# One set of phase multiples, high rows by turning forward and back, late numerators copied by ScalarE, and spectra of u in two-bank PSUM tiles

## The chip, the cores and the metric

The kernel runs on one core of one Trainium2 chip. The metric is the device time of one execution in microseconds: the median of three runs of the kernel before is 298.48 us (298.02 to 301.67). Beside the runs there is one profiled execution with a trace of every instruction; it took 299.34 us and its span, from the first to the last instruction, is 297.6 us. The core's engines are TensorE (PE, whose weight loads are listed as PEld), VectorE (DVE), ScalarE (ACT), GpSimd (POOL) and SyncE (SP); the last two do little but issue transfers here. Each engine works through its own list of instructions in order and waits on semaphores for the others.

## The reference

Two independent parts are computed, and their outputs stand side by side in one array of 2048 x 896 in bf16.

Part A is linear attention with feature maps: sequence length 2048, width 448, 16 heads of 28.

```
q, k, v = split(x @ wqkv)
phi_q = [softmax(q @ w_phi), softmax(-(q @ w_phi))]      # the same for phi_k
kv, z   = phi_k^T v, sum of phi_k over the sequence
o       = (phi_q kv) / (phi_q z + 1e-6);   out_A = o @ wo
```

Part B is a state-space convolution: 448 channels, 256 states, length 2048.

```
K[d, l] = Re sum_n C[d, n] exp(dt[d] A[d, n] l) dt[d] B[d, n]       # l = 0 .. 2047
y       = causal convolution of u with K along l, by FFT of length 4096;  out_B = y + u * Dskip
```

## The kernel before

**The table of powers.** The 448 channels are cut into 8 chunks (k = 0 to 7) of 56. In a chunk 128 states lie on partitions, and a row has 112 columns: 56 channels by two halves of the states (`COLS`). The kernel K is evaluated only at such l as bf16 can hold, each as a sum of a high part from `HI` (32 values: multiples of 32 up to 1920) and a low part from `LO` (50 values between -15 and 128). For each chunk the steps are:

- `phases` (L663): PE multiplies the log-magnitudes (`AT`) or the angles (`TH`), as bf16 pairs of value and remainder, with scaled identities (`PID`), one for each entry of `DIAG`. There are two sets of eight multiples, so two PSUM tiles of two banks (`arg`, of which two exist) for the magnitudes and two for the angles, each by 16 matmuls of 128x112. ACT then evaluates groups of rows out of PSUM by `EVALS` and, for the negative rows, `MIRROR`: `dampings` takes exponentials into `E` (11 instructions, 49 rows), `rotations` takes sines and cosines into `W` (16 instructions, 2 x 34 rows). The scale of an instruction (1, 2, 4, 8) turns one set of multiples into others.
- `damp` (L700): DVE multiplies the rotations with the exponentials, in two pieces (3360 and 7616 columns); `neg` flips a sign in 1680 columns, on DVE or ACT.
- `hi_tables` (L714): DVE builds the 32 high rows in `U`, as complex products in bf16. Rows 0 to 3 are copied from `H`. Level 1 multiplies them by the 128th power (rows 4 to 7), level 2 all eight by the 256th power (rows 8 to 15), and levels 3 to 5 use the 512th. A level is one multiply of both factors' parts at once, then a subtraction and an addition.
- `build_k` (L734): PE contracts `U` with `W` into PSUM, and ACT or DVE copies the result into a table of K values.

`W`, `E` and `U` have two buffers, so a chunk's work overlaps that of the next two.

**From the table to the output.** DMAs scatter the table into rows by position (`scatter_k`, issued on SP, POOL and ACT), PE transforms it (`kernel_spectrum`, with tables that are loaded from DRAM by `load_f` into a ring of buffers, and copies by ACT or DVE into `SK`), DVE multiplies it with the spectrum of u (`conv_group`), and PE transforms back (`inverse`), for three channel groups one after the other: group 0 is chunks 0 to 3, group 1 chunks 4 and 5, group 2 chunks 6 and 7. The spectrum of u is computed early (`signal_spectrum`, L621): in steps of 448 columns it is transformed into one-bank PSUM tiles (`mm`), copied by ACT or DVE, and sent to DRAM (`SUd`); `load_su` brings it back, one load for each group.

**Attention.** `key_pair` and `key_end` build kv and z. `query` (L808) handles four blocks of 512 positions, sc = 0 to 3. For each of a block's four tiles PE makes the numerators of both softmax halves in a two-bank `arg` tile, DVE multiplies them out of PSUM (f32) by the scale `SC`, one factor for each head of 28 columns, into `on` (bf16, 896 columns), and PE adds the halves, transposes and projects.

**What sets the order.** Every operation is a unit with its engines and dependencies. Nothing is scheduled at build time: the string `ORDER` (L98) lists all 1451 units, each with the engine that issues it (P, V, A, G and S for PE, DVE, ACT, POOL and SP), and `PLACES` (L168) says which PSUM pool a tile comes from. An engine's list is the order of its units in that string. Copies, sign flips and transfers may stand on either of several engines. The costs written beside the units were used to find the string and change nothing else.

## Time and profile before

| | |
|---|---|
| Median of three runs | 298.48 us (298.02 to 301.67) |
| Profiled execution | 299.34 us, span 297.6 us |
| PE busy | 263.8 us (89% of the span) |
| DVE busy | 275.7 us (93%) |
| ACT busy | 247.4 us (83%) |
| POOL busy | 71.5 us (24%) |
| Transfers | 35.20 MB, mean 118 GB/s |
| Granted TensorE clock | 0.992 |

Busy time is the time in which at least one instruction of the engine runs. An instruction's own duration includes the wait for its last results, which overlaps the next instruction on the same engine; the sum of durations is therefore more than the busy time. In a row of a group stand, after the bar, the busy time, the mean duration of one instruction, and the idle time of the engine before them with what ended it. Line numbers are those of the helpers that issue: L345 is `tt` (two-operand DVE work), L358 is `act` (activations), L362 is `acopy`, L368 is `copy`, L378 is `mm`, L393 is `dma`, L712 is the sign flip.

### The profile page before, as it was taken

The page shows a single profiled execution, that of the slowest core. Times are in us where ns is not written, and L with a number is a line of the kernel's source. Part 1 is how long each engine was busy: PE and PEld are TensorE (multiplying, and loading weights), DVE is VectorE, ACT ScalarE, POOL GpSimd, SP SyncE. Part 2 cuts the span into 40 slices and gives each one's busy share as a digit, 9 for nine tenths or more (in the row PEclk, how much of TensorE's full clock was granted, in tenths as well). Part 3 has the DMA queues.
Part 4 walks back from the last instruction along what each step waited for, and adds up shares of the span by engine and source line. Part 5 has one row for each costly group of instructions (what it writes and reads, how often), then busy time and mean ns, then how long its engine had stood idle before and what let it go on. Part 6 is the DMA issues. An engine that isn't in the chain of part 4 may idle for free. (4 is left out here: it accounts for less than half of the span.)

```text
span 297.6 us, 10488 instructions
## 1 busy us (share of the span) xinstructions
PE 263.8 (89%) x4536; PEld 215.4 (72%) x4536; DVE 275.7 (93%) x317; ACT 247.4 (83%) x470; POOL 71.5 (24%) x123
## 2 busy tenths in 40 slices
PE   7788999999989899989997879899778889899994
PEld 3455676786685687868775659688667688889983
DVE  2799999999999999899999999899989999999990
ACT  2989999999999999999699999999999825452331
POOL 4031222502011101000298000029910048600000
PEclk9999999999999999999997999999999999999998
DMA  6976544542022101021044300316986878775025
GB/s 197 315 207 199 165 103 133 117 65 54 10 67 50 45 4 46 4 48 50 6 69 84 85 17 4 87 43 130 261 303 175 256 232 220 196 244 173 18 79 170
DMA packets 40520, 35.20 MB, mean 118 GB/s; under 512 B 22078, under 2 KB 37687, under 8 KB 40347
## 3 DMA queue, kind: packets, MB, share of 16 engines
q1 hardware_dynamic: 34999, 30.53, 35.1%
q0 software_dynamic: 4288, 3.97, 6.8%
q8 instruction: 35, 0.57, 0.8%
q10 hardware_dynamic: 1188, 0.04, 0.2%
q14 instruction: 10, 0.08, 0.1%
HBM read 24.28 MB, written 7.34 MB: 106 GB/s over the span
## 5 line engine op out<-in xcount | busy, mean ns | idle before, releaser
L378 PEld LDWEIGHTS <-sbuf 128*32 128x32 bf16 (+4 forms) x4312 | 203.8, 118 | 70.8 <-issue 32.6
L345 DVE TENSOR_TENSOR sbuf<-sbuf 128x896 bf16<-128x896 bf16 (+6 forms) x197 | 216.7, 1135 | 5.6 <-ACT sbuf L358 4.1
L378 PE MATMUL mm<-sbuf 128*32 128x50 bf16 (+10 forms) x2257 | 143.8, 267 | 14.6 <-ACT sbuf L368 6.5
L358 ACT ACTIVATE sbuf<-arg 128x448 bf16<-128x448 f32 (+4 forms) x238 | 125.9, 644 | 1.4 <-PE arg L378 0.7
L378 PE MATMUL kb<-sbuf 128*32 128x50 bf16 (+9 forms) x1153 | 74.3, 246 | 3.4 <-ACT sbuf L368 1.0
L393 POOL DMA_DIRECT2D sbuf<-sbuf x80 | 47.8, 623 | 113.3 <-ACT sbuf L368 95.6
L378 PE MATMUL arg<-sbuf 128*128 128x112 bf16 (+4 forms) x902 | 62.4, 220 | 7.7 <-ACT sbuf L358 5.9
L368 ACT CAST sbuf<-mm 128x448 bf16<-128x448 f32 (+4 forms) x96 | 54.3, 585 | 16.7 <-PE mm L378 14.5
L368 ACT CAST sbuf<-kb 128x448 bf16<-128x448 f32 (+3 forms) x42 | 23.3, 593 | 19.3 <-PE kb L378 16.1
L393 POOL DMA_DIRECT2D SUd<-sbuf x24 | 17.9, 749 | 61.5 <-ACT sbuf L368 42.9
L358 ACT ACTIVATE sbuf<-mm 112x512 bf16<-112x512 f32 x36 | 21.2, 649 | 0.3 <-PE mm L378 0.3
L345 DVE TENSOR_TENSOR sbuf<-arg,sbuf 128x896 bf16<-128x896 f32 (+1 forms) x21 | 20.3, 973 | 0.6 <-PE mm L378 0.2
L358 ACT ACT_TABLE_LOAD x14 | 18.0, 1283 | 1.4 <-PEq L1106 1.2
L358 ACT ACTIVATE sbuf<-sbuf 128x896 f32<-128x896 f32 (+2 forms) x12 | 11.7, 1017 | 1.8 <-DMA sbuf<-in_B_log_dt_dram 1.8
L712 ACT ACTIVATE sbuf<-sbuf 128x1680 bf16<-128x1680 bf16 x6 | 10.5, 1756 | 0.0
L785 PEld LDWEIGHTS <-sbuf 112*128 112x128 bf16 x128 | 7.3, 97 | 1.8 <-issue 1.0
L368 DVE COPY sbuf<-kb 112x512 bf16<-112x512 bf16 (+2 forms) x16 | 6.8, 434 | 1.4 <-PE kb L574 0.9
L345 DVE TENSOR_TENSOR sbuf<-mm,sbuf 128x896 bf16<-128x896 bf16 (+1 forms) x13 | 7.4, 566 | 0.6 <-PE mm L785 0.5
L368 DVE CAST sbuf<-mm 128x448 bf16<-128x448 f32 (+1 forms) x11 | 6.6, 597 | 1.0 <-PE mm L378 0.7
L574 PEld LDWEIGHTS <-sbuf 128*112 128x112 bf16 x64 | 4.9, 129 | 3.3 <-issue 2.8
L574 PE MATMUL kb<-sbuf 128*112 128x128 bf16 x64 | 5.7, 219 | 1.7 <-ACT sbuf L368 1.5
L362 ACT CAST sbuf<-sbuf 128x1792 bf16<-128x1792 f32 (+1 forms) x5 | 7.1, 1429 | 0.0
(37 smaller groups left out, 63.3 us busy)
## 6 DMA issues: line engine op xcount, KB each, us to landing
sbuf<-const SPq DMA_DIRECT2D x36, 224.0 KB
sbuf<-const SPq DMA_DIRECT2D x7, 512.0 KB
sbuf<-in_B_u_dram SPq DMA_DIRECT2D x6, 448.0 KB
sbuf<-in_A_x_dram SPq DMA_DIRECT2D x4, 448.0 KB
out_dram<-sbuf SPq DMA_DIRECT2D x16, 112.0 KB
sbuf<-SUd SPq DMA_DIRECT2D x1, 1792.0 KB
sbuf<-SUd SPq DMA_DIRECT2D x2, 896.0 KB
out_dram<-sbuf SPq DMA_DIRECT2D x8, 224.0 KB
```

Source lines behind the costliest of these rows:

```text
L345: lambda: nc.vector.tensor_tensor(out=at(out_), in0=at(a), in1=at(b), op=op), [whose(a), whose(b)], [out_])
L358: lambda: nc.scalar.activation(at(out_), at(a), func, scale=scale, bias=bias),
L362: plan.add({"ACT": 0.09 + count(out_) * 0.833e-3}, lambda: nc.scalar.copy(at(out_), at(a)), [whose(a)], [out_])
L368: lambda e: (nc.scalar.copy if e == "ACT" else nc.vector.tensor_copy)(at(out_), at(a)), [whose(a)], [out_])
L378: nc.tensor.matmul(out_, lhsT=lhsT, rhs=rhs, start=start, stop=stop, **kw)
L393: plan.add({e: own[e] for e in engs}, lambda e=engs[0]: QUEUES[e].dma_start(out=out_, in_=in_, **kw), r, w, lat=lat, load=pieces / 16000 * ...
L574: mms(p, [lambda t, j=j, x=x: nc.tensor.transpose(t[:, j, :], x[:, 112 * j:112 * j + 112], ident[:, :]) for j in range(4)], 0.4, [x, ident ...
L712: lambda en: nc.scalar.mul(m, m, -1.0) if en == "ACT" else nc.vector.tensor_scalar_mul(m, m, -1.0), [m], [m])
L785: mms(pt, [lambda t, i=i, s=s, c=c: nc.tensor.transpose(t[:, s, 112 * c:112 * c + 112], EKT[:, s, c, 128 * i:128 * i + 128], id112) for s ...
```

## The change

- `phases` uses one set of eight multiples (1, 3, ... 15) in one PSUM tile. The other rows come from larger scales of the instructions on ACT (up to 128), in more and shorter groups: 15 exponentials and 2 x 11 sines for a chunk.
- `hi_tables` first makes rows 8 to 11 from rows 0 to 3 by the 256th power. A second product of these four rows with the 128th power serves twice: with one set of signs it gives rows 12 to 15 and, turned the other way, rows 4 to 7, which are then scaled by the new tile `BACK` (the inverse of the squared magnitude, made once at the start).
- In `query`, blocks from `N_EARLY` = 2 on take another way: ACT copies the numerators out of PSUM into `on`, and DVE multiplies `on` in place by a bf16 scale.
- `signal_spectrum` uses two-bank `arg` tiles of 2 x 448 columns, with one copy each.
- The order of all units (now 1517) and the places of the PSUM tiles are new, and with them the engine of many copies, sign flips and transfers. `gather` has other costs written beside it.

```diff
--- before.py
+++ after.py
@@ -21,6 +21,7 @@
 SSM_N = 256
 
 N_IDLE = 24
+N_EARLY = 2
 N_LO = 50
 N_HI = 32
 NQ = 14
@@ -30,17 +31,15 @@
 QC = 2 * COLS
 NCOL = NCHK * COLS
 HW = D_MODEL // 2
-DIAG = [[1, 3, 5, 7, 9, 11, 13, 15], [4, 8, 12, 16, 20, 28, 24, 32]]
-EVALS = [[(1, 0, 8, 16, 2, 0), (2, 0, 4, 17, 4, 0), (4, 4, 2, 34, 1, 0), (8, 4, 4, 42, 2, 0)],
-         [(1, 0, 4, 19, 4, 0), (1, 4, 4, 32, 1, 1), (2, 4, 4, 38, 1, 2), (4, 4, 4, 43, 2, 2)]]
-MIRROR = [[(-1, 0, 8, 0, 2, 0), (-2, 0, 4, 1, 4, 0)], [(-1, 0, 3, 3, 4, 0)]]
+DIAG = [1, 3, 5, 7, 9, 11, 13, 15]
+EVALS = [(1, 0, 8, 16, 2), (2, 0, 4, 17, 4), (4, 0, 2, 19, 8), (4, 2, 4, 32, 1), (8, 0, 1, 23, 1), (8, 1, 7, 38, 1),
+         (16, 0, 2, 31, 5), (16, 2, 2, 45, 1), (32, 0, 2, 37, 10), (64, 0, 1, 48, 1), (128, 0, 1, 49, 1)]
+MIRROR = [(-1, 0, 8, 0, 2), (-2, 0, 4, 1, 4), (-4, 0, 2, 3, 8), (-8, 0, 1, 7, 1)]
 ZERO = 15
 LO = [0] * N_LO
-for _ds, _ev, _mi in zip(DIAG, EVALS, MIRROR):
-    for _f, _e, _n, _r, _s, _kind in _ev + _mi:
-        for _i in range(_n):
-            _j = (_i, 4 * (_i // 2) + _i % 2, 2 * (_i % 2) + _i // 2)[_kind]
-            LO[_r + _s * _j] = _f * _ds[_e + _i]
+for _f, _e, _n, _r, _s in EVALS + MIRROR:
+    for _i in range(_n):
+        LO[_r + _s * _i] = _f * DIAG[_e + _i]
@@ -89,85 +88,88 @@
...
-ORDER = ("23G 42P 31P 43P 30P 33P 46P 0A 48A 49V 8G 191G 32..."
...
-PLACES = ("kmmmmkmmkmmkmmkkmkkmkkmkkkkkmmkmmkmmkkmkmkmmmkkk..."
...
+ORDER = ("0A 48A 3S 1S 2S 4S 8G 23G 13S 25P 46P 36P 30P 32P..."
...
+PLACES = ("kkkkmmkkkmkmmkmmkmmmmkkmmkkmmmkkmmamkkmmakmkakak..."
...
@@ -398,12 +400,13 @@
     oEND = oF + 61672
     oT2 = oEND + 4096
     DSK = sb("DSK", [128, D_MODEL], BF16, oDSK)
-    PID = sb("PID", [128, 16, 128], BF16, oPID)
+    PID = sb("PID", [128, 8, 128], BF16, oPID)
     H = sb("H", [128, 4, 2, NCOL], BF16, oH)
     AT = sb("AT", [128, 2, NCOL], BF16, oAT)
     TH = sb("TH", [128, 2, NCOL], BF16, oTH)
     PW = {k: sb(f"PW{k}", [128, 2, NCOL], BF16, o) for k, o in
           ((32, oEND), (64, oF + 16384), (128, oPW), (256, oPW + 3584), (512, oPW + 7168))}
+    BACK = sb("BACK", [128, NCOL], BF16, oPID + 2048)
@@ -522,6 +525,10 @@
     phase = step("amp", 14, 0)
     for k in LOWP:
         act(amp[k][:, :], fs[0][:, :], ACT.Exp, phase, scale=float(k))
+    grow = sb("grow", [128, NCOL], F32, oW + 37632)
+    plan.add({"DVE": 0.6}, lambda: nc.vector.tensor_scalar(grow[:, :], fs[0][:, :], -256.0, 69.0, op0=ALU.mult, op1=ALU.min),
+             [fs[0][:, :]], [grow[:, :]])
+    act(BACK[:, :], grow[:, :], ACT.Exp, phase)
     step("hl", 16)
     for f, hl in zip(fs, (AT, TH)):
         acopy(hl[:, 0, :], f[:, :])
@@ -607,9 +614,9 @@
 
 
     def gather(out_, src, rows):
-        plan.add({"POOL": 1.5}, lambda: nc.gpsimd.indirect_dma_start(
+        plan.add({"POOL": 1.15}, lambda: nc.gpsimd.indirect_dma_start(
             out=out_.rearrange("p t d -> p (t d)"), out_offset=None, in_=src.rearrange("(q t) d -> q (t d)", t=4),
-            in_offset=bass.IndirectOffsetOnAxis(ap=rows, axis=0)), [rows], [out_], lat=3.5, load=1.6)
+            in_offset=bass.IndirectOffsetOnAxis(ap=rows, axis=0)), [rows], [out_], lat=7.0, load=1.6)
 
     def by_quarter(t):
         return t.rearrange("p (g q x) -> p q g x", g=4, q=4)
@@ -640,15 +647,15 @@
                     step(f"us{b}.{i}", rank)
                     sg = sgs[i % 2]
                     i += 1
+                    p = ps("arg", [128, 2, 512])
                     for k2 in range(2):
                         mt = 2 * mp + k2
-                        p = ps("mm", [128, 512])
-                        mms(p, [lambda t, jt=jt, mt=mt, cp=cp, st_=st_: mm(
-                            t[:, 0:D_MODEL].rearrange("p (q g x) -> p q g x", q=4, g=4),
+                        mms(p, [lambda t, jt=jt, mt=mt, cp=cp, st_=st_, k2=k2: mm(
+                            t[:, k2, 0:D_MODEL].rearrange("p (q g x) -> p q g x", q=4, g=4),
                             G1[:, cp, jt, 128 * mt:128 * mt + 128], by_quarter(sums[cp ^ st_][:, jt, :]),
                             jt == 0, jt == 3) for jt in range(4)], 0.77,
                             [G1[:, cp, :, 128 * mt:128 * mt + 128], sums[cp ^ st_]])
-                        copy(sg[:, k2, :], (p, lambda t: t[:, 0:D_MODEL]))
+                    copy(sg[:, :, :], (p, lambda t: t[:, :, 0:D_MODEL]))
                     for gi, (q0, nq) in enumerate(GROUPS):
                         part = sg[:, :, 112 * q0:112 * (q0 + nq)]
                         dma(["SP", "POOL"], SUd[gi][:, b, cp, st_, 2 * mp:2 * mp + 2, :], part, r=[part],
@@ -661,33 +668,23 @@
             pool(0.2, lambda par=par, c=c: nc.gpsimd.memset(W[:, par, c, ZERO, :], 1.0 - c), [], [W[:, par, c, ZERO, :]])
 
     def phases(src, k, phase, use, evals):
-        for d in range(2):
-            p = ps("arg", [128, 2, 512], order=phase)
-            mms(p, [lambda t, e=e, d=d, part=part: mm(
-                t[:, e // 4, (e % 4) * COLS:(e % 4 + 1) * COLS], PID[:, 8 * d + e, :], src[:, part, k * COLS:(k + 1) * COLS],
-                part == 0, part == 1) for e in range(8) for part in range(2)], 0.8,
-                [PID[:, 8 * d:8 * d + 8, :], src[:, :, k * COLS:(k + 1) * COLS]])
-            for f, e, n, r, s, kind in evals[d]:
-                def rows(t, skip=0, n=n, r=r, s=s, kind=kind):
-                    r = r - skip if r > ZERO else r
-                    if kind == 1:
-                        return t[:, r:r + 8, :].rearrange("p (a b) x -> p a b x", a=2)[:, :, 0:2, :]
-                    v = t[:, r:r + (n - 1) * s + 1:s, :]
-                    return v.rearrange("p (b a) x -> p a b x", a=2) if kind else (
-                        v.rearrange("p (a b) x -> p a b x", a=2) if n == 8 else v)
-
-                def view(t, e=e, n=n, kind=kind):
-                    v = t[:, :, 0:4 * COLS].rearrange("p a (b x) -> p a b x", b=4)
-                    if n == 8:
-                        return v
-                    v = v[:, e // 4, 0:n, :]
-                    return v.rearrange("p (a b) x -> p a b x", a=2) if kind else v
-                use(rows, (p, view), float(f))
+        p = ps("arg", [128, 2, 512], order=phase)
+
+        def at_(t, e, n):
+            return t.rearrange("p a b -> p (a b)")[:, 512 - 4 * COLS + e * COLS:512 - 4 * COLS + (e + n) * COLS]
+        mms(p, [lambda t, e=e, part=part: mm(at_(t, e, 1), PID[:, e, :], src[:, part, k * COLS:(k + 1) * COLS],
+                                             part == 0, part == 1) for e in range(8) for part in range(2)], 0.8,
+            [PID[:, :, :], src[:, :, k * COLS:(k + 1) * COLS]])
+        for f, e, n, r, s in evals:
+            def rows(t, skip=0, n=n, r=r, s=s):
+                r = r - skip if r > ZERO else r
+                return t[:, r:r + (n - 1) * s + 1:s, :]
+            use(rows, (p, lambda t, e=e, n=n: at_(t, e, n).rearrange("p (b x) -> p b x", x=COLS)), float(f))
 
     def dampings(k, rank, phase):
         phase = step(f"exps{k}", rank, phase)
         phases(AT, k, phase, lambda rows, src, f: act(rows(E[:, k % 2], 1), src, ACT.Exp, phase, scale=f),
-               [a + b for a, b in zip(EVALS, MIRROR)])
+               EVALS + MIRROR)
 
     def rotations(k, rank, phase):
         phase = step(f"rot{k}", rank, phase)
@@ -716,20 +713,34 @@
         cols = slice(k * COLS, (k + 1) * COLS)
         u = U[:, k % 2]
         dma(["SP", "POOL"], u[:, 0:4], H[:, :, :, cols], r=[H[:, :, :, cols]], w=[u[:, 0:4]])
-        for lv, (j, dst, src, n) in enumerate(((128, u[:, 4:8], H[:, :, :, cols], 4), (256, u[:, 8:16], u[:, 0:8], 8),
-                               (512, u[:, 16:24], u[:, 0:16:2], 8), (512, u[:, 24:28], u[:, 16:24:2], 4),
-                               (512, u[:, 28:32], u[:, 24:28], 4))):
+        def times(j, src, n):
+
+            t2 = sb("t2", [128, 2, n, 2, COLS], BF16, oT2)
+            if src is H:
+                wide = t2.rearrange("p b n r x -> p b (n r) x")
+                both = src[:, :, :, cols].rearrange("p n r x -> p (n r) x").unsqueeze(1).to_broadcast([128, 2, 2 * n, COLS])
+            else:
+                wide, both = t2, src.unsqueeze(1).to_broadcast([128, 2, n, 2, COLS])
+            tt(wide, both, PW[j][:, :, cols].unsqueeze(2).to_broadcast([128, 2, 2 * n, COLS]), ALU.mult)
+            return t2
+        for lv, (j, dst, src, n) in enumerate(((256, u[:, 8:12], H, 4), (128, None, u[:, 8:12], 4),
+                                               (512, u[:, 16:24], u[:, 0:16:2], 8), (512, u[:, 24:28], u[:, 16:24:2], 4),
+                                               (512, u[:, 28:32], u[:, 24:28], 4))):
             step(f"hi{k}.{lv + 1}", rank)
-            t2 = sb("t2", [128, 2, n, 2, COLS], BF16, oT2)
-            if lv:
-                wide, both = t2, src.unsqueeze(1).to_broadcast([128, 2, n, 2, COLS])
+            t2 = times(j, src, n)
+            if dst is None:
+                uf = u.rearrange("p n r x -> p (n r) x")
+                a, b = (t2[:, i].rearrange("p n r x -> p r n x") for i in range(2))
+
+                def pair(first, gap):
+                    v = uf[:, first:first + gap + 7]
+                    return bass.AP(tensor=v.tensor, offset=v.offset, ap=[v.ap[0], [gap * COLS, 2], [2 * COLS, 4], [1, COLS]])
+                tt(pair(9, 15), a[:, ::-1], b, ALU.subtract)
+                tt(pair(8, 17), a, b[:, ::-1], ALU.add)
+                tt(uf[:, 8:16], uf[:, 8:16], BACK[:, cols].unsqueeze(1).to_broadcast([128, 8, COLS]), ALU.mult)
             else:
-                wide = t2.rearrange("p b n r x -> p b (n r) x")
-                both = src.rearrange("p n r x -> p (n r) x").unsqueeze(1).to_broadcast([128, 2, 2 * n, COLS])
-            tt(wide, both,
-               PW[j][:, :, cols].unsqueeze(2).to_broadcast([128, 2, 2 * n, COLS]), ALU.mult)
-            tt(dst[:, :, 0], t2[:, 0, :, 0], t2[:, 1, :, 1], ALU.subtract)
-            tt(dst[:, :, 1], t2[:, 0, :, 1], t2[:, 1, :, 0], ALU.add)
+                tt(dst[:, :, 0], t2[:, 0, :, 0], t2[:, 1, :, 1], ALU.subtract)
+                tt(dst[:, :, 1], t2[:, 0, :, 1], t2[:, 1, :, 0], ALU.add)
 
     def build_k(k, Ts, x0, rank):
         for hq in range(2):
@@ -826,7 +837,8 @@
         rz = sb("rz", [128, 4, 2, 16], F32, oRZ)
         dz = sb("dz", [128, 4, 2, 16], F32, oRZ + 512)
         den = sb("den", [128, 2, 4, 16], F32, oRZ + 1024)
-        SC = sb("SC", [128, 4, 2, 16], F32, oSC, bufs=2)
+        late = sc >= N_EARLY
+        SC = sb("SCb", [128, 4, 2, 16], BF16, oSC + 256 * (sc % 2)) if late else sb("SC", [128, 4, 2, 16], F32, oSC + 512 * (sc % 2))
         plan.add({"DVE": 0.87}, lambda: nc.vector.reciprocal(rz[:, :, :, :], at(ndv(1))), [pz], [rz[:, :, :, :]])
         tt(dz[:, :, :, :], ndv(0), rz[:, :, :, :], ALU.mult)
         stt(den[:, 0], dz[:, :, 0, :], 1e-6, dz[:, :, 1, :], ALU.add, ALU.add)
@@ -841,8 +853,10 @@
                                                        True, True) for c in range(4)], 0.22,
                     [EQ[:, s, :, ts], KVN[:, s]])
             on = sb("on", [128, 2, D_MODEL], BF16, oON, bufs=2)
-            tt(on.rearrange("p s (h d) -> p s h d", d=D_HEAD),
-               (pn, lambda t: t[:, :, 0:D_MODEL].rearrange("p s (h d) -> p s h d", d=D_HEAD)),
+            heads = on.rearrange("p s (h d) -> p s h d", d=D_HEAD)
+            if late:
+                acopy(on[:, :, :], (pn, lambda t: t[:, :, 0:D_MODEL]))
+            tt(heads, heads if late else (pn, lambda t: t[:, :, 0:D_MODEL].rearrange("p s (h d) -> p s h d", d=D_HEAD)),
                SC[:, t4].unsqueeze(3).to_broadcast([128, 2, 16, D_HEAD]), ALU.mult)
             po = ps(("mm", "kb"), [112, 4, 128])
             mms(po, [lambda t, c=c, s=s, on=on: mm(t[:, c, :], on[:, s, 112 * c:112 * c + 112], ident[:, :], s == 0, s == 1)
```

More of the change, by code (lines that the diff above doesn't have):

```diff
@@ L91, in _dft_tables @@
     FT = FT.reshape(7, 128, 16, 128).transpose(2, 1, 0, 3)
-    pid = np.eye(128)[:, None, :] * np.array(DIAG).reshape(-1)[None, :, None]
+    pid = np.eye(128)[:, None, :] * np.array(DIAG)[None, :, None]
     hm = np.zeros((112, 4, D_HEAD + 1))
@@ L96, in _dft_tables @@
     return tuple(_round_bf16(t) for t in (G, GI, FT, pid, hm))
-ORDER = ("23G 42P 31P 43P 30P 33P 46P 0A 48A 49V 8G 191G 32P 45P 38P 3S 1S 17G 2S 19G 6S 190S 50V 51V 53V 52V 56P 57V 54P "
[69 rows of a table removed]
-PLACES = ("kmmmmkmmkmmkmmkkmkkmkkmkkkkkmmkmmkmmkkmkmkmmmkkkmkmkkmmkkmkkmamkamkkmmkkkmaamkmakammakammkmkmmkkmmakkmmammmmamam"
-         "mmmammmmammmamamammammmammammmmammmmammmmmmamamaamamaamammmmammaammaamamammmkakmkammakakmakkmakammkaaakamkakmamk"
-         "kmammaakkmkmkmaakkmmaamkmkaamkkaamkakmamkaakmkmkakmmmkkkmkmmkamkamkmmmmkkamkmmkmmmakmmmkmkmmakkkka")
+ORDER = ("0A 48A 3S 1S 2S 4S 8G 23G 13S 25P 46P 36P 30P 32P 47P 44P 29P 17G 193G 27P 49V 50V 53V 51V 192S 19G 52V 54P 55V "
[72 rows of a table added]
+PLACES = ("kkkkmmkkkmkmmkmmkmmmmkkmmkkmmmkkmmamkkmmakmkakakmamkkmkmkkmaakkmmkakammkkmkmkmkmkmkmmkkmamamammmmammmmmmmmammamm"
+         "ammmaamammmaammmammmmmmammamammmmmaaamammmmmamakmmkkammakakakkmakkmmamakakmmkkakkmaakkakmmkkkmkmamkkamkkmakkmmkm"
+         "mamaakkkakkmkkmkmmaamkmkmmkakkmkmamakkmmkkmkkkmmaammkkmkkmkakkakaa")
 ENGINES = {"P": "PE", "V": "DVE", "A": "ACT", "G": "POOL", "S": "SP"}
```

141 rows, old and new, of the table ORDER are left out of this document.

## Prediction

> **What bounds the kernel now.** I read the page's busy shares and slices first, to see which engine is never free.
>
> ```profile
> PE 263.8 (89%) x4536; PEld 215.4 (72%) x4536; DVE 275.7 (93%) x317; ACT 247.4 (83%) x470; POOL 71.5 (24%) x123
> DVE  2799999999999999899999999899989999999990
> ACT  2989999999999999999699999999999825452331
> ```
>
> VectorE (DVE) is full from the second slice to the last but one. ScalarE (ACT) is full until slice 31 and half idle after it. To size this I cut the span in four with the view of windows: the head, the front (up to the last damping multiply of chunk 7), the tail, and what is left when VectorE has finished.
>
> ```profile
> 0.00:32.00 32.00, 26.65 (x202) 15.86 (x203) 24.54 (x43) 25.29 (x35) 8.40 (x17) 1.00 0.79 230
> 32.00:231.90 199.90, 179.61 (x3324) 145.95 (x3322) 192.62 (x232) 195.58 (x378) 48.78 (x81) 0.99 0.32 82
> 231.90:291.00 59.10, 55.37 (x971) 51.56 (x971) 58.54 (x43) 25.50 (x57) 14.28 (x25) 1.00 0.60 178
> 291.00:297.60 6.60, 2.22 (x46) 2.05 (x42) 0.00 (x0) 1.06 (x2) 0.00 (x0) 0.87 0.44 147
> ```
>
> After the length come PE, PEld, DVE, ACT and POOL. In the front ACT lacks 4.3 us of 199.9 and DVE 7.3: both are bounds there. In the tail DVE lacks 0.56 us of 59.1 while ACT is free for 33.6: VectorE alone sets it. The last 6.6 us are the final inverse transform and its store. The timeline of DVE shows the seam between front and tail:
>
> ```profile
> 220.93 10.80 DVE L345 TENSOR_TENSOR sbuf<-sbuf 128x7616 bf16<-128x7616 bf16 x10
> 231.91 4.12 DVE L345 TENSOR_TENSOR sbuf<-sbuf 128x7616 bf16<-128x7616 bf16 x1 [0.17 <-ACT sbuf L358]
> ```
>
> The multiply at 231.91 waited 0.17 us for ACT's last sine. The two lists run level and meet there, so the change is worth, in the front, what it takes off the longer of the two lists, and in the tail what it takes off DVE. PE, at 89%, is late for DVE only in short gaps.
>
> **What one instruction costs.** A group's mean includes an end that overlaps the next instruction, so I take the distance between starts from timelines:
>
> ```profile
> 243.69 1.08 DVE L345 TENSOR_TENSOR sbuf<-arg,sbuf 128x896 bf16<-128x896 f32 x1
> 244.69 13.49 DVE L345 TENSOR_TENSOR sbuf<-sbuf 128x1792 bf16<-128x1792 bf16 x5
> 87.56 3.69 ACT L358 ACTIVATE sbuf<-arg 128x448 bf16<-128x448 f32 x8
> 90.96 0.71 ACT L368 CAST sbuf<-mm 128x448 bf16<-128x448 f32 x1
> 96.89 0.98 ACT L358 ACTIVATE sbuf<-arg 128x896 bf16<-128x896 f32 x1
> 97.70 0.60 ACT L368 CAST sbuf<-mm 128x448 bf16<-128x448 f32 x1
> 78.40 0.36 ACT L358 ACTIVATE sbuf<-arg 128x224 bf16<-128x224 f32 x1
> 78.66 0.96 ACT L368 CAST sbuf<-mm 128x448 bf16<-128x448 f32 x2
> ```
>
> On DVE 1.08 us costs 1.00: I take 0.08 off each mean below. On ACT eight activations of 448 columns take 3.40 us, 0.425 each; one of 896 takes 0.81; one of 224 takes 0.26. From the first two, 448 columns cost 0.385 and an instruction about 0.05 by itself (0.04 to 0.07 over the three).
>
> **The change, part by part.**
>
> ```profile
> L345 DVE TENSOR_TENSOR sbuf<-sbuf 128x3584 bf16<-128x3584 bf16 x28 | 56.5, 2019 | 0.3
> L345 DVE TENSOR_TENSOR sbuf<-sbuf 128x1792 bf16<-128x1792 bf16 x39 | 41.8, 1077 | 0.2
> L345 DVE TENSOR_TENSOR sbuf<-sbuf 128x896 bf16<-128x896 bf16 x50 | 29.3, 613 | 0.4
> L345 DVE TENSOR_TENSOR sbuf<-arg,sbuf 128x896 bf16<-128x896 f32 x16 | 17.2, 1083 | 0.5 <-PE mm L378 0.2 <-PE arg L378 0.2
> L345 DVE TENSOR_TENSOR sbuf<-mm,sbuf 128x896 bf16<-128x896 bf16 x11 | 6.8, 618 | 0.6 <-PE mm L785 0.5
> L368 DVE CAST sbuf<-mm 128x448 bf16<-128x448 f32 x10 | 6.2, 618 | 1.0 <-PE mm L378 0.7
> L368 ACT CAST sbuf<-mm 128x448 bf16<-128x448 f32 x67 | 39.7, 607 | 12.1 <-PE mm L378 11.7 <-issue 0.3
> L358 ACT ACTIVATE sbuf<-arg 128x448 bf16<-128x448 f32 x152 | 78.5, 611 | 1.0 <-PE arg L378 0.7
> L712 ACT ACTIVATE sbuf<-sbuf 128x1680 bf16<-128x1680 bf16 x6 | 10.5, 1756 | 0.0
> L712 DVE TENSOR_SCALAR sbuf<-sbuf 128x1680 bf16<-128x1680 bf16 x2 | 1.2, 618 | 0.0
> L368 ACT CAST sbuf<-mm 128x350 bf16<-128x350 f32 x12 | 7.0, 587 | 0.5 <-PE mm L378 0.5
> L378 PE MATMUL arg<-sbuf 128*128 128x112 bf16 x584 | 34.3, 213 | 4.7 <-ACT sbuf L358 3.4 <-DVE sbuf L345 1.3
> ```
>
> *High rows (DVE, all in the front).* Each of 8 chunks loses a multiply of 3584 columns (1.94) and gains one of 1792 (1.00) and one of 896 (0.53, the turn's rescaling); its two additions of 896 stay. 8 x (1.00 + 0.53 - 1.94) = -3.3 us. The reversed halves and the rows written in pairs still end in 112 adjacent columns, as in the rows above.
>
> *One set of multiples.* PE loses 32 of 64 phase matmuls per chunk: 256 at 34.3/584 = 0.059, 15 us of PE. It bounds no stretch, so I book nothing; what it may return is a rival below. On ACT the elements stay the same, in smaller pieces: 11 exponentials and 16 sines per chunk become 15 and 22, 80 instructions more, at 0.055 each 4.4 us. Ten of a chunk's 37 have only 112 columns, a size no row shows: between 0.10 (columns alone) and 0.26 (the row of 224). I take 0.15, by the fixed part that three sizes agree on; the upper end would add 80 x 0.11 = 9 us. The Trainium skill, "ScalarE: Activation LUTs", section "What ACT_TABLE_LOAD costs", gives 186 ns + 0.833 ns a column, of which some 93 ns overlap: 0.47 us for 448 columns. The trace has 0.425 and decides; by the page the 80 would cost 7.4 us.
>
> *Late numerators.* For the last two of four query blocks (8 tiles) ACT copies 896 columns out of PSUM (0.81 each) and DVE multiplies the bf16 copy. What that multiply costs, no row shows directly. The two nearest are the same multiply today, 1.00 (the x16 row, whose scale is one element standing for 28 neighbours), and bf16 multiplies at 0.54 (the x11 row, whose scale changes with every column). The new one shares the data type with the second and the scale's pattern with the first. I take 1.00, since every fast row has operands that step from element to element: so nothing is won per tile on DVE. The Trainium skill weighs in here against the change: "VectorE: DVE Perf Modes", section "What auto-detection actually checks", wants 16-bit tensors with step ±1 for the double rate, and "Vector Engine (DVE) Microarchitecture Reference", section 5.1, found a two-source op that reads one element 16 times at the single rate. No run here shows it yet; by these pages the tile costs 1.00 as well.
>
> *Spectra of u.* 32 copies of 448 become 16 of 896. ACT goes from 28 copies (28 x 0.42 = 11.8) to 15 (12.2), DVE from 4 (4 x 0.54) to 1 (1.00): +0.4 and -1.2. They now take the two-bank buffers in which the phases and numerators stand; there are two, and the cover is that ACT empties them in list order.
>
> *The new order.* It shifts work that either engine may do; I counted both orders. In the front DVE gets 3 more sign flips (+1.6; ACT -3 x 1.5 = -4.5), 5 table copies (0.44 each, +2.2; ACT -4 x 0.36), 3 kernel-spectrum copies (+1.6; ACT -5 x 0.42, two of them moved to the tail) and the growth factor (0.6; between 0.1 and the 1.00 of a single-rate 896); ACT gets its exponential (0.85). Table loads stay at 14.
>
> **Sums.** DVE front: high rows -3.3, flips +1.6, table copies +2.2, spectrum copies +1.6, u copies -1.2, growth +0.6, numerators (14 before the seam, then 8 plain and 3 late, all at 1.00) -3.0, a few small copies, mostly of 448, -0.7: **-2.2 us**. ACT front: pieces +4.4, flips -4.5, table copies -1.4, spectrum copies -2.1, u copies +0.4, three late copies +2.4, exponential +0.85, projection copies -2.1: **-2.1 us**. Both shrink alike, so the seam comes 2.1 us earlier. DVE tail: 5 late multiplies against 2 plain ones, at 1.00, +3.0, and output copies +0.1: **+3.1 us**. ACT's tail gains some 5 us under 33 idle ones: hidden. Head and final 6.6 us I take as they are. Total -2.2 + 3.1 = +0.9: 299.34 us of the profiled execution (297.6 of span) become 300.2. That execution lies 0.9 above the median 298.48 of the runs, so I forecast **299.4 us**, no change to speak of.
>
> **Rivals.**
> *Fast multiply.* If the scale's pattern does not matter, 8 x 0.46 = 3.7 us go: 295.7.
> *The gaps close.* DVE's 7.3 us of front gaps partly wait on PE and on ACT behind PE; 15 us less PE work may close half, 295.8, and all with a denser order, 292.1. Against it: ACT lacks only 4.3 us there.
> *ACT overflows.* (the other side) If a 112-column activation occupies ACT like one of 224, the ACT front becomes -2.1 + 9 = +7 while DVE's is -2.2. With the lists level today every 0.1 us counts from the first; the seam moves +7, with the tail +3.1: 309; at half that price +2.4 and +3.1: 304.
> *A late load.* Before conv group 2, DVE needs its u spectrum from DRAM:
>
> ```profile
> 258.99 0.46 SPq L393 DMA_DIRECT2D sbuf<-SUd  x1
> 261.66 6.73 SPq L393 DMA_DIRECT2D sbuf<-const  x7
> 277.43 2.02 DVE L345 TENSOR_TENSOR sbuf<-sbuf 128x3584 bf16<-128x3584 bf16 x1
> 259.00:273.00 14.00, 13.46 (x206) 12.77 (x204) 13.91 (x13) 5.70 (x14) 0.00 (x0) 1.00 0.79 246
> ```
>
> Today that load (0.92 MB) is issued at 258.99, 18 us before the multiply at 277.43, ahead of the seven transform tables. In the new order it stands on SP's queue behind the last of them, whose issue waits for PE to free a buffer (268.4 today). At 246 GB/s it takes 3.7 us, behind three tables (0.7 MB, 2.8 us): landing near 275 against a need near 278. If sharing or SP's waits cost over 3 us more, DVE stalls for the rest; 3 to 5 us give 302 to 304.5.
>
> **How the numbers follow.** Forecast 0.44 (297 to 302), fast multiply 0.10, gaps 0.20, overflow 0.10, late load 0.16. A measurement of this kernel tells about 2% (6 us) from no change. Over 2% faster means below 292.5: half of the gap case, and it together with the fast multiply, 0.12. Over 2% slower means above 304.5: the overflow and the worst of the late load, 0.16. Between them 0.72. The range 293 to 305.5 leaves out the far ends of gaps and overflow.
>
> **What would show it.** The eight late multiplies: a DVE group "sbuf<-sbuf 128x896" near 1.08 us (right) or near 0.61 (fast). The activations of 112 columns: start-to-start 0.15. The multiplies of 3584 in bf16: 20, not 28. DVE's idle time ended by ACT before the last damping multiply near 230 us. No DVE gap before the first conv-2 multiply. The prediction is wrong if VectorE's busy time falls by more than 4 us, or if its idle time moves by more than 3.

## The result and the profile after

The median after is 296.31 us (294.11 to 299.17, 18 runs), beside 299.63 us (298.02 to 304.6, 18 runs) of the kernel before, measured side by side. The ratios, here and below, leave out single slow runs, over 1.5% above the fastest of their kernel (here the one of 299.17 us), which the medians contain. The ratio is 0.987, with a 95% interval from 0.9844 to 0.9896: 1.3% faster, a small gain, but a sure one. The forecast of 299.4 us, no change to speak of, missed it. The profiled execution took 295.46 us, 3.9 us less than the one before, and its span is 293.7 us.

The busy shares and slices of the page after:

```profile
PE 252.4 (86%) x4280; PEld 203.5 (69%) x4280; DVE 275.4 (94%) x334; ACT 249.6 (85%) x535; POOL 70.6 (24%) x119
DVE  2799999999999999999999999999999999999980
ACT  3999999999999999999999999999999467533421
```

VectorE is busy for the same 275.4 us as before (275.7), in a shorter span. The digits of 8 in the middle of its line are gone, and ScalarE shows no digit below 9 until slice 31. So the time did not come out of VectorE's work as a whole, but out of its idle time. The view of windows, first before and then after, is cut at the start of the last damping multiply (the seam, 231.9 and 223.07) and at VectorE's last product (290.51 and 284.9). After the length come PE, PEld, DVE, ACT and POOL, then the granted TensorE clock, the DMA share and GB/s:

```profile
231.90:290.51 58.61, 54.88 (x961) 51.07 (x961) 58.23 (x43) 25.50 (x57) 14.28 (x25) 1.00 0.60 177
290.51:297.60 7.09, 2.71 (x56) 2.54 (x52) 0.30 (x2) 1.06 (x2) 0.00 (x0) 0.88 0.47 160
```

```profile
0.00:32.00 32.00, 25.49 (x188) 14.01 (x189) 25.11 (x41) 26.38 (x33) 7.10 (x16) 0.95 0.80 223
32.00:223.07 191.07, 164.42 (x3040) 131.79 (x3038) 188.65 (x248) 190.20 (x438) 48.37 (x77) 1.00 0.33 83
223.07:284.90 61.83, 57.78 (x986) 53.33 (x984) 60.93 (x47) 31.61 (x65) 15.16 (x26) 0.97 0.58 173
284.90:293.70 8.80, 4.66 (x78) 4.41 (x75) 0.69 (x3) 1.41 (x3) 0.00 (x0) 0.92 0.41 138
```

The terms of the sum, as forecast and as measured:

| | forecast | measured |
|---|---|---|
| Seam | -2.1 us | -8.8 us (231.9 to 223.07) |
| Seam to VectorE's last product | +3.1 | +3.2 (58.61 to 61.83; the clock was 1.00 and 0.97) |
| From there to the end | 0 | +1.7 (7.09 to 8.80) |
| Sum | +0.9 | -3.9 |

The front, up to the seam, carries the miss. From 32 us on VectorE lacked 7.3 us there before and lacks 2.4 now (191.07 - 188.65); in the head it lacks 0.6 less. That is 5.4 us less idle time. Its busy time up to the seam falls by 3.4 us (24.54 + 192.62 before, 25.11 + 188.65 after). I had -2.2. Counted group by group at the distances between starts, the work falls by some 3.6 us: high rows -3.2, flips +1.6, numerators -3.0 and growth +0.5 are as forecast, but the copies and the other small instructions give +0.5 where the sum had +1.9. ScalarE's busy time up to the seam falls by 4.3 us (25.29 + 195.58 before, 26.38 + 190.20 after), beside -2.1 in the sum; at the distances between starts its work falls by some 1.6, and the rest of the 4.3 are the ends of instructions beside gaps that have closed, and short delays, which the records count as busy. Its idle time falls by 4.5.

The waits in the front say whose gaps they were. First before, up to 231.9 us: VectorE's longest entry, and ScalarE's four (the columns are the total, the number and the longest):

```profile
DVE sbuf L345 <- ACT sbuf L358: 3.9, 7, 0.8
...
ACT sbuf L358 <- PE kb L378: 1.9, 1, 1.9
ACT sbuf L358 <- PE arg L378: 0.7, 1, 0.7
ACT sbuf L368 <- PE mm L378: 0.5, 1, 0.5
ACT sbuf L358 <- PE mm L378: 0.3, 1, 0.3
```

The same after, up to 223.07 us:

```profile
DVE sbuf L347 <- ACT sbuf L360: 0.4, 2, 0.2
...
ACT sbuf L370 <- PE kb L380: 0.3, 1, 0.3
ACT sbuf L360 <- PE arg L380: 0.2, 1, 0.2
```

VectorE waited for ScalarE's sines and exponentials, 3.9 us, and ScalarE for PE, 3.4 us. Both waits have all but gone. They were not one chain throughout: before, ScalarE's waits for PE end between 145 and 167 us, while VectorE's for ScalarE end at 85, 107, 126, 171, 184, 187 and 218 us. Between 32 us and the third of these ScalarE had no gap over 0.05 us, so there its full list was late, and not PE. That is the rival I had called "The gaps close", with 295.8 to 292.1 us for it.

### The profile page after: what moved, and what is told of

The parts are those of the page before. It is cut to its first block, busy times and chain, and to the rows that moved or that the text cites. A ratio compares the mean times of both kernels' runs of the same rounds, so it can differ in the third digit from the quotient of the medians.

```text
span 293.7 us, 10074 instructions
## 1 busy us (share of the span) xinstructions
PE 252.4 (86%) x4280; PEld 203.5 (69%) x4280; DVE 275.4 (94%) x334; ACT 249.6 (85%) x535; POOL 70.6 (24%) x119
## 4 chain that ended last, share of the span: by engine, by line
ACT 36%; DVE 36%; PE 13%; issue 6%; DMA 5%; SPq 3%; ACTq 0%; DVEq 0%
DVE sbuf L347 30%; ACT sbuf L360 28%; ACT sbuf L370 5%; PE mm L380 5%; PE kb L380 4%; PE arg L380 4%; DMA sbuf<-in_A_wqkv_dram 3%; DVE sbuf L370 3%; SPq L395 3%; ACT L360 2%; DMA sbuf<-sbuf 2%; DVE sbuf L351 1%; DVE sbuf L842 1%; ACT sbuf L709 1%; DVE sbuf L845 0%
## 5 line engine op out<-in xcount | busy, mean ns | idle before, releaser
L380 PEld LDWEIGHTS <-sbuf 128*32 128x32 bf16 (+4 forms) x4056 | 190.7, 119 | 78.5 <-issue 38.4
L347 DVE TENSOR_TENSOR sbuf<-sbuf 128x896 bf16<-128x896 bf16 (+9 forms) x213 | 221.1, 1079 | 2.3 <-ACT sbuf L364 0.7
L380 PE MATMUL mm<-sbuf 128*32 128x50 bf16 (+11 forms) x1901 | 110.4, 261 | 18.1 <-ACT sbuf L360 6.0
L360 ACT ACTIVATE sbuf<-arg 128x224 bf16<-128x224 f32 (+5 forms) x302 | 121.2, 664 | 0.3 <-PE arg L380 0.2
L380 PE MATMUL kb<-sbuf 128*32 128x50 bf16 (+9 forms) x1457 | 81.7, 247 | 7.5 <-issue 2.6
L380 PE MATMUL arg<-sbuf 128*128 128x112 bf16 (+4 forms) x698 | 69.4, 249 | 7.9 <-ACT sbuf L360 4.7
L395 POOL DMA_DIRECT2D sbuf<-sbuf x77 | 46.5, 633 | 103.8 <-issue 38.1
L370 ACT CAST sbuf<-mm 128x448 bf16<-128x448 f32 (+4 forms) x53 | 33.9, 671 | 11.1 <-PE mm L380 7.0
L370 ACT CAST sbuf<-kb 128x448 bf16<-128x448 f32 (+3 forms) x46 | 27.9, 645 | 15.7 <-PE kb L380 14.8
L395 POOL DMA_DIRECT2D SUd<-sbuf x23 | 16.7, 726 | 72.7 <-ACT sbuf L370 69.8
L360 ACT ACTIVATE sbuf<-mm 112x512 bf16<-112x512 f32 x46 | 28.1, 711 | 0.1
L370 ACT CAST sbuf<-arg 128x896 bf16<-128x896 f32 (+2 forms) x27 | 19.4, 747 | 6.4 <-PE arg L380 4.4
L360 ACT ACTIVATE sbuf<-sbuf 128x896 f32<-128x896 f32 (+3 forms) x13 | 12.6, 1013 | 1.9 <-DMA sbuf<-in_B_log_dt_dram 1.9
L347 DVE TENSOR_TENSOR sbuf<-arg,sbuf 128x896 bf16<-128x896 f32 (+1 forms) x10 | 9.7, 988 | 0.1
L364 ACT CAST sbuf<-arg 128x896 bf16<-128x896 f32 x8 | 8.3, 1052 | 1.0 <-PE arg L380 0.9
L347 DVE TENSOR_TENSOR sbuf<-mm,sbuf 128x896 bf16<-128x896 bf16 (+1 forms) x15 | 8.8, 593 | 0.1
L796 PE MATMUL mm<-sbuf 112*128 112x112 bf16 x112 | 7.8, 212 | 1.1 <-ACT sbuf L370 0.6
L364 ACT CAST sbuf<-sbuf 128x1792 bf16<-128x1792 f32 (+1 forms) x5 | 7.2, 1430 | 0.0
L360 ACT ACTIVATE sbuf<-kb 112x512 bf16<-112x512 f32 x12 | 7.0, 667 | 0.0
L370 DVE CAST sbuf<-arg 128x224 bf16<-128x224 f32 (+1 forms) x4 | 2.2, 560 | 4.8 <-ACT sbuf L370 4.8
```

Of the source, the lines that this page charges most:

```text
L347: lambda: nc.vector.tensor_tensor(out=at(out_), in0=at(a), in1=at(b), op=op), [whose(a), whose(b)], [out_])
L360: lambda: nc.scalar.activation(at(out_), at(a), func, scale=scale, bias=bias),
L364: plan.add({"ACT": 0.09 + count(out_) * 0.833e-3}, lambda: nc.scalar.copy(at(out_), at(a)), [whose(a)], [out_])
L370: lambda e: (nc.scalar.copy if e == "ACT" else nc.vector.tensor_copy)(at(out_), at(a)), [whose(a)], [out_])
L380: nc.tensor.matmul(out_, lhsT=lhsT, rhs=rhs, start=start, stop=stop, **kw)
L395: plan.add({e: own[e] for e in engs}, lambda e=engs[0]: QUEUES[e].dma_start(out=out_, in_=in_, **kw), r, w, lat=lat, load=pieces / 16000 * ...
```

## Experiments

The helpers of the kernel after stand two lines lower than before: L347 is `tt`, L360 `act`, L364 `acopy`, L370 `copy`, L380 `mm`, L395 `dma`. Differences are taken between kernels that were measured together; where medians and ratios to before give different ones, both stand. The mark for the first group is the kernel after once more:

> The changed kernel once more, on the chip of the next three, as their reference: a ratio of 0.985 to 0.990 to the kernel before, VectorE idle for about 4 us between its first work and the last damping multiply (9.3 us before).

It took 295.75 us, 0.9846 of before (0.9801 to 0.9891).

**PE's work put back.** Every phase matmul is issued twice, so that a chunk has 64 again:

```diff
-  part == 0, part == 1) for e in range(8) for part in range(2)], 0.8,
+  part == 0, part == 1) for again in range(2) for e in range(8) for part in range(2)], 0.8,
```

> The changed kernel with every phase matmul issued twice into the same tile: the 256 matmuls (15 us of TensorE) that the change took away are back, all else is the same. Theory PE (the gaps of VectorE closed because TensorE had less to do): the gaps return, 3 to 5 us more than the changed kernel, ratio near 1.00. Theory ORDER (they closed because the new order keeps both lists fed): less than 1 us more, ratio 0.985 to 0.991.

Measured: 299.37 us, 0.998 of before (0.9954 to 1.0007): 3.6 us more than the mark by the medians, 4.0 by the ratios, and the whole gain gone. No instruction of VectorE or ScalarE differs. The windows of this kernel, cut at its own seam:

```profile
32.00:227.54 195.54, 176.22 (x3297) 145.45 (x3296) 189.35 (x249) 191.92 (x438) 48.36 (x77) 0.99 0.32 81
227.54:288.70 61.16, 55.66 (x979) 51.66 (x977) 60.94 (x47) 30.83 (x63) 15.16 (x26) 1.00 0.60 176
288.70:297.50 8.80, 4.66 (x78) 4.41 (x75) 0.69 (x2) 1.41 (x3) 0.00 (x0) 0.98 0.41 138
```

The seam is 4.5 us later than after (227.54 beside 223.07), while tail and end are no longer than after. VectorE lacks 6.2 us of the front in place of 2.4. The waits in this front, VectorE's longest three and ScalarE's longest:

```profile
DVE sbuf L347 <- PE mm L796: 1.0, 2, 0.8
DVE sbuf L347 <- PE kb L380: 0.9, 1, 0.9
DVE sbuf L347 <- ACT sbuf L360: 0.7, 3, 0.3
...
ACT sbuf L360 <- PE arg L380: 2.0, 4, 1.0
```

The 256 matmuls, which I had booked at nothing, cost some 4 us of time through gaps of the engines that wait for PE. Most of VectorE's waits name PE itself here, and not ScalarE.

**PE's work taken out of the kernel before.** Here the phases of the kernel before leave out the matmuls of the bf16 remainders (256 fewer; the angles lose their second half, so this kernel computes less):

```diff
-  part == 0, part == 1) for e in range(8) for part in range(2)], 0.8,
+  True, True) for e in range(8) for part in range(1)], 0.8,
```

> The kernel before, without the phase matmuls of the remainders (half of 512; the bf16 remainders of magnitudes and angles are left out, so its output is less exact); the order is the old one. Theory PE: TensorE is relieved as by the change, VectorE's gaps close, 3 to 4 us less than before, ratio 0.987 to 0.990. Theory ORDER: under 1 us less.

Measured: 300.04 us, 0.9998 of before (0.9965 to 1.003). The window that ends at the seam of before shows PE's load fall and nothing follow:

```profile
32.00:231.90 199.90, 171.52 (x3071) 135.25 (x3070) 192.48 (x233) 195.30 (x378) 50.10 (x82) 0.98 0.32 82
```

PE has 8.1 us less than before in it, VectorE and ScalarE have 192.5 and 195.3, as before. This execution is the slowest of the twelve (302.51 us), and its own seam is at 233.06; from 32 us up to there VectorE lacks 7.6 us and ScalarE 4.6 (7.3 and 4.3 before), and ScalarE still waits 3.6 us for PE. So relief of PE shortens neither engine's waits and brings no time in the old order, beside some 4 us in the new one. My reason for it, which no run shows: an instruction still stands at its old place in each engine's list, and what it waits for is issued no earlier. Two things limit the comparison. The phases here still fill two `arg` tiles for each set, where the change fills one. And the mean granted clock of the twelve executions was 0.978, beside 0.989 in those of the kernel before next to them; over all its runs 0.01 of clock goes with some 1.2 us of time, so about 1 us of gain may be hidden, by an estimate from these runs.

**High rows as before.** The old five levels, 3.3 us more VectorE work by my sum; for five chunks the copy of rows 0 to 3 is issued earlier, since the old first addition needs its place.

```diff
-  ((256, u[:, 8:12], H, 4), (128, None, u[:, 8:12], 4),
+  ((128, u[:, 4:8], H, 4), (256, u[:, 8:16], u[:, 0:8], 8),
```

> The changed kernel with the high rows made as before (first by the 128th, then all eight by the 256th power, no rescaling): VectorE has 8 x 0.41 = 3.3 us more in the front. If VectorE's list bounds the front: 2.5 to 3.5 us more than the changed kernel, ratio 0.996 to 0.999. If ScalarE's list bounds it (it was idle 1.8 us there against VectorE's 4.0): under 1 us more.

Measured: 296.70 us, 0.9886 of before (0.9852 to 0.992): 0.95 us above the mark by the medians, 1.2 by the ratios, with overlapping intervals. Its seam is 3.1 us later than after (226.15 beside 223.07, both read from the records) and its span 2.3 us longer (296.0 beside 293.7). The direction is as expected, but the size lies nearer to the under 1 us that I expected if ScalarE's list bounds the front than to the 2.5 to 3.5 us if VectorE's does; the intervals do not settle it.

**No late copies.** All four query blocks take the numerators straight out of PSUM. On VectorE the multiply costs the same 1.08 us; ScalarE is spared eight copies.

```diff
-N_EARLY = 2
+N_EARLY = 4
```

> The changed kernel without the eight late copies: all numerators are multiplied out of PSUM in f32 as before, at the same places of the order. VectorE's multiply took 1.08 us after the copy as before it, so the theory (no gain on VectorE) has no change, within 1 us. Rival (the copy frees the two-bank PSUM tile early, and TensorE with it): 1.5 to 3 us more than the changed kernel.

Measured: 303.45 us, 1.0119 of before (1.0076 to 1.0163), 7.7 us above the mark by the medians, 8.2 by the ratios. Its seam is at 230.03, 7.0 us later than after. The waits of this kernel up to its seam, for VectorE, ScalarE and PE in turn:

```profile
DVE sbuf L347 <- ACT sbuf L360: 6.5, 4, 4.7
...
ACT sbuf L360 <- PE arg L380: 7.9, 2, 7.7
...
PE arg L380 <- DVE sbuf L347: 7.7, 2, 6.5
```

The timeline shows the ring that they form, one row of each of VectorE, PE, ScalarE and VectorE:

```profile
218.53 1.09 DVE L347 TENSOR_TENSOR sbuf<-arg,sbuf 128x896 bf16<-128x896 f32 x1
...
219.67 2.51 PE L380 MATMUL arg<-sbuf 128*128 128x112 bf16 x24 [6.47 <-DVE sbuf L347]
...
221.36 2.19 ACT L360 ACTIVATE sbuf<-arg 128x224 bf16<-128x224 f32 x5 [7.66 <-PE arg L380]
...
226.88 2.51 DVE L347 TENSOR_TENSOR sbuf<-sbuf 128x3360 bf16<-128x3360 bf16 x3 [4.66 <-ACT sbuf L360]
```

A tile of numerators sits in one of the two `arg` buffers until VectorE, which comes to it only after the damping of the chunk before, has multiplied it at 218.53. Until then PE cannot write the next phases (6.47 us), so ScalarE has no angles (7.66 us), so VectorE has no sines (4.66 us). ScalarE's copy takes VectorE out of this ring. That is what the late copies are worth in this order, which was made with them (the kernel before does without them in its own), and it has nothing to do with the price of the multiply, over which the prediction deliberated.

**The order alone.** All three undone at once (phase matmuls twice, old high rows, no late copies), in the new order:

> The changed kernel with three parts undone together: phase matmuls issued twice, high rows as before, no late copies. What is left of the change is the order, the shorter activations and the two-bank spectra of u. Theory ORDER: 3.3 us more than the changed kernel (VectorE's high rows alone), ratio 0.998. Theory PE: 7 us more, ratio above 1.008.

Measured: 311.7 us, 1.0393 of before (1.0349 to 1.0437). The new order with these three parts of the old work is far worse than the kernel before. The longest entry of VectorE's waits in its front:

```profile
DVE sbuf L347 <- ACT sbuf L360: 8.9, 6, 6.1
```

Parts and order belong together: neither this order without the three parts nor PE's relief in the old order gains any time. By the ratios it stands 5.5% of before above the mark of the first group, 16 us; undone one by one, the three cost 4.0, 1.2 and 8.2 us, 13.4 in sum. The intervals of these ratios taken together leave some 3.5 us of room, so it is not settled whether each makes the others' absence worse.

**Pieces in the kernel before.** The price of 80 more activations, tried in the old order: 80 of its activations of 448 columns are cut in two.

> The kernel before, with 80 of its phase activations cut in two (ten for a chunk, as many instructions more as the change brings): ScalarE has 80 x 0.055 = 4.4 us more in the front. If the two lists are level there, as the prediction says: 3 to 4.4 us more, ratio 1.010 to 1.015. If ScalarE has slack: under 1 us.

Measured: 302.8 us, 1.0089 of before (1.0056 to 1.0123): 2.8 us (1.7 to 3.7 by the interval) of the 4.4 that the sum has for them. ScalarE's list did bound the front before, so most of the price in the sum is a real one, and the new order had to win it back.

**The fast multiply.** With the columns of the numerators in the order channel, head, the scale steps from element to element. The rows of `wo` must then be permuted, which I did by four loads in place of one, each over every fourth partition:

```diff
-  KVN = sb("KVN", [112, 2, 4, 4, D_HEAD], BF16, o1)
+  KVN = sb("KVN", [112, 2, 4, D_HEAD, 4], BF16, o1)
...
-  dma(["SP"], wo[:, :, :], A_wo.rearrange("(c p) n -> p c n", p=112), w=[wo[:, :, :]])
+  nc.sync.dma_start(out=wo[hh:112:4, :, :], in_=A_wo.rearrange("(c h d) n -> h d c n", c=4, h=4)[hh])   # hh = 0 to 3
...
+  scale = SC[:, t4].rearrange("p s (c h) -> p (s c) h", h=4).unsqueeze(2).to_broadcast([128, 8, D_HEAD, 4])
```

> The changed kernel with the numerators' columns in the order channel-then-head (kv and the rows of wo permuted), so that the scale of the late multiply changes from column to column: its eight multiplies should take 0.62 us in place of 1.08, 3.7 us less on VectorE, 2.3 of it in the tail. Theory VectorE bounds the tail: 2 to 3.5 us less than the changed kernel, ratio 0.976 to 0.980. Theory TensorE bounds the tail (idle for 4 of 62 us there): under 1 us less.

Measured: 304.07 us, 1.0119 of before (1.0066 to 1.0172), beside 0.987 after: some 7 us slower than after. VectorE's longest wait in this kernel:

```profile
DVE sbuf L347 <- DMA sbuf<-in_A_wo_dram: 5.3, 1, 5.3
```

The instruction that waits, at 67.08 us, is a multiply of 896 columns with an operand out of the PSUM pool `mm`, which reads nothing of `wo`. I took it for a matter of SP's queue, and moved the four loads later, to a quiet stretch, beside a kernel with the old load and a new mark:

> The kernel after once more, as the mark for the three beside it: 0.987 of before, 296 us.

> The same column order, but with the rows of wo permuted to match by four loads instead of one, now issued on SP some 45 us later, in its quiet stretch near 103 us and before the first projection near 160 us. Theory load (the 5 us that VectorE waited near 67 us with the early four loads were their place in SP's queue): as the run with the plain load, within 0.5 us. Rival: four loads over 28 partitions each cost in any place: 2 us or more above it.

> The kernel after, with the numerators' columns in the order channel, head, so that the scale steps from element to element; wo is loaded as before, so the projection uses its rows in the wrong order (the output of part A is not the reference's, the work is the same). Theory VectorE (it alone sets the tail): the eight late multiplies go from 1.08 to 0.61 us; five of them lie in the tail, 5 x 0.47 = 2.3 us off, and with the three in the front at most 3.7: 292.4 to 293.8. Rival PE (PE has only 3.7 idle us of the tail's 61.8 and takes over at the end): under 1 us, 295.2 to 296.1.

The mark took 295.91 us (0.9861 of before, 0.9818 to 0.9904). With the four loads later: 301.51 us (1.0024, 0.9991 to 1.0057), 5.6 us above the mark by the medians, so my theory of the place in the queue fell. The wait moved with the loads and grew; now a damping multiply waits, at 114.73 us:

```profile
DVE sbuf L347 <- DMA sbuf<-in_A_wo_dram: 7.9, 1, 7.9
```

PE and ScalarE wait for the same loads at the same time (4.5 and 4.0 us near 114 us). Three engines that need nothing of `wo` stop for it, in both places. It looks as if the build takes a view of every fourth partition to touch more than it does and orders other work behind it; I have not shown that, and a load of the same rows in another way was not tried.

With the plain load (the projection then takes the rows of `wo` in the wrong order, so part A of the output is not the reference's) there is no such wait, and the multiply can be read alone. The group of 896 columns in bf16, after and then in this kernel:

```profile
L347 DVE TENSOR_TENSOR sbuf<-sbuf 128x896 bf16<-128x896 bf16 x66 | 43.3, 674 | 1.4 <-ACT sbuf L364 0.7
```

```profile
L347 DVE TENSOR_TENSOR sbuf<-sbuf 128x896 bf16<-128x896 bf16 x66 | 39.6, 617 | 2.0 <-ACT sbuf L364 1.4
```

The 66 instructions include the eight late ones, at 1.08 to 1.09 us each after; with them at the rate of the others the mean falls from 674 to 617 ns, 3.7 us in all. Yet the time is 295.40 us (0.9815, 0.9757 to 0.9873), 0.5 us below the mark by the medians and 1.4 by the ratios, which the scatter does not resolve. The tails, of the mark and then of this kernel:

```profile
222.87:283.88 61.01, 56.73 (x986) 52.12 (x984) 60.84 (x47) 31.48 (x65) 15.21 (x26) 1.00 0.61 179
```

```profile
222.50:283.64 61.14, 58.43 (x992) 54.19 (x992) 58.77 (x45) 32.40 (x66) 15.17 (x26) 0.97 0.61 176
```

VectorE's busy time in the tail falls by 2.1 us and the tail is no shorter: the difference comes back as idle time, and PE lacks only 2.7 us of it. But the two tails ran at granted clocks of 1.00 and 0.97. The tail after, above, also ran at 0.97: it took 61.83 us for the same 986 matmuls, with PE busy for 57.78 in place of 56.73, and beside it this tail is 0.7 us shorter. The two kernels with four loads have the same fast multiply in the tail; theirs take 59.99 us at 1.00 and 60.59 at 0.97. So at an equal clock 2.1 us less on VectorE bring 0.7 to 1.2 us: after, PE shares in setting the tail. Before, VectorE alone set it in the profiled execution, at 1.00; the same tail at 0.97 took 60.64 and 61.89 us in the kernels without remainders and with pieces, VectorE being busy for 58.4 and 58.3.

**The end.** Of the last inverse tile, 18 matmuls that the new order leaves behind all others, 14 are left out, and with them a part of the output:

```diff
+  if (gi, b, r, jp) == (0, 1, 1, 4 // per - 1):
+      calls = [calls[i] for i in (0, 8, 9, 17)]
```

> The kernel after, with 14 of the 18 matmuls of the very last inverse tile (group 0, second block) left out, so a part of the output is not computed. Theory end (behind VectorE's last result, PE's backlog sets the time until the store): 14 x 0.1 = 1.4 us off, 294.7. Rival store (the last store and its wait set it, PE does not): 0, 296.1.

Measured: 295.42 us, 0.9812 of before (0.9762 to 0.9862), 0.5 us below the mark by the medians and 1.5 by the ratios, which the scatter does not resolve. The traces do. PE's last groups and VectorE's last copy, after and then with the short tile:

```profile
285.91 3.66 PE L380 MATMUL arg<-sbuf 128*128 128x112 bf16 x54
...
289.98 0.39 DVE L370 CAST sbuf<-arg 128x224 bf16<-128x224 f32 x1 [4.78 <-ACT sbuf L370]
```

```profile
287.06 2.32 PE L380 MATMUL arg<-sbuf 128*128 128x112 bf16 x40
...
289.84 0.39 DVE L370 CAST sbuf<-arg 128x224 bf16<-128x224 f32 x1 [3.49 <-ACT sbuf L370]
```

From 284.1 us on PE works without a gap until the last copies, and 14 matmuls less make VectorE's wait before the last one 1.3 us shorter (4.78 to 3.49). From VectorE's last product to the end this kernel takes 7.5 us, after 8.8. So PE's backlog, not the store alone, makes the end longer: 1.3 of the 1.7 us are shown to be its own.

Undoing the two-bank spectra of u by themselves was not tried.

## Why the prediction was wrong, step by step

- **VectorE's front work, -2.2 us: right in its large parts, some 1.4 us short in the small ones.** -3.4 was measured as busy time, -3.6 by the distances between starts; the copies and small instructions make the difference. The multiplies of 3584 columns are 20 as forecast (mean 2013 ns).
- **80 activations at 0.055 more each, 112 columns at 0.15: right.** The group after is

```profile
L360 ACT ACTIVATE sbuf<-arg 128x112 bf16<-128x112 f32 x80 | 31.4, 447 | 0.0
```

  and its records start 0.143 us (median) after one another, which is below the middle of the 0.10 to 0.26 that I had. The Trainium skill, "ScalarE: Activation LUTs", section "What ACT_TABLE_LOAD costs", would make it 186 + 0.833 x 112 - 93 = 186 ns, an estimate by that page; the trace has 143. ScalarE did not overflow.
- **The late multiply at the single rate: right.** 1.08 us with the repeated scale, 0.61 with one that steps. The Trainium skill, "VectorE: DVE Perf Modes", section "What auto-detection actually checks", grants the double rate to 16-bit tensors that all have step ±1; here both sides of it are measured. But I priced only the multiply of the late numerators, and missed what their copy frees: the `arg` tile.
- **The tail, +3.1 us: right in kind, and near in number by luck** (+3.2). VectorE's busy time grew by 2.7 us (58.23 to 60.93). The tail before ran at a clock of 1.00, the one after at 0.97; the mark's tail at 1.00 took 61.01 us, which is +2.4. "VectorE alone sets it" holds for before at that clock; after, PE shares in it.
- **"It bounds no stretch, so I book nothing", on PE's 15 us: the step that failed.** PE is never the longest list, and yet its relief is worth some 4 us in this order. I took the front as the work of the longer list plus gaps that stay, and the gaps did not stay: 5.4 us of VectorE's idle time went. Three parts of the change take part in that: less PE work (some 4 us when it is put back), copies that free the tile early (some 8 us when they are left out), and an order built on both. Which of the old waits each part removed is not shown; some had PE behind them, others a full ScalarE. Of the 7.3 us of gaps in the front I had none closing in the forecast, and half or all in a rival with a chance of 0.20. The argument against that rival, that ScalarE lacks only 4.3 us, was weak: by my own sum ScalarE's list shrank by 2.1 us besides, and it lacks 0.9 now.
- **"Head and final 6.6 us I take as they are": wrong by +1.7 us in the end.** The timeline of PE at the end of the new order would have been the place to ask; the order alone, which was open to reading, shows an inverse tile of group 0 as the very last unit.
- **A late load of u's spectrum: did not come.** There is no gap of VectorE before the first product of group 2.
- **The signs.** I had said that VectorE's idle time ends by ScalarE before the last damping multiply, and that the prediction is wrong if the idle time moves by more than 3 us. The first was not there (no gap at 223.07), the second happened.

## What to carry to other kernels

When two engines run level with short gaps that name each other and a third engine, the gaps are a term of the sum: follow each wait back one step further, and ask which part of the change cuts that chain, even if the engine at its root is idle a tenth of the time. A PSUM buffer is held until its last reader is done, so who reads it decides more than what the read costs; a copy by an engine that comes by early can pay for itself though no instruction gets cheaper. And relief of an engine off the longest list was worth time here only together with an order that uses it. Before two stretches of single executions are compared, their granted clocks must be: 0.03 of clock went with 0.8 us of the same tail after, and with 2 us or more before.

## What was not expected of the hardware

- A multiply whose second operand repeats each element 28 times takes 1.08 us for 896 bf16 columns, and 0.61 with the same data in an order in which it steps by one; the change of layout alone sets it.
- Activations out of PSUM start 0.143, 0.237, 0.423 and 0.797 us apart for 112, 224, 448 and 896 columns: close to 0.05 us and 0.83 ns a column at all four sizes. Out of SBUF 896 columns take 0.84 to 0.86.
- Four loads of `wo` over every fourth partition were followed by waits of 5.3 and 7.9 us on engines that do not use it. The cause is open.
